# Evacuating transposed tiles on two engines, with one store of x per chunk, fewer halo copies and another load order

## The chip, the cores and the metric

One core of a Trainium2 chip runs the whole program. The metric is the device time of one execution in microseconds (us). The engines are named as in the profile: PE multiplies matrices and writes to PSUM, DVE (vector), ACT (scalar) and POOL (GpSimd) work element by element, and POOL and SP issue most DMAs. To evacuate a tile is to copy it out of PSUM. Most executions of a kernel lie within some 0.3% of each other, so every time below is set against runs of the kernel before on the same chip.

## The reference, cut to what matters

```python
x = causal_depthwise_conv(x_in, softmax(weight))   # 7 taps, 8 heads of 24 channels
theta = x @ w_theta                                # per token, 192 x 192
zr, zi = x * cos(theta), x * sin(theta)
y = w_tok_r @ zr + w_tok_i @ zi                    # over 4224 tokens: nearly all the work
u = x + y
out = u + relu(u @ w_ch)                           # per token, 192 x 192
```

Sizes: batch 8, 4224 tokens, 192 channels.

## The kernel before

The 4224 tokens are cut into 33 chunks of 128. A chunk is made ready as follows: load (`xw`), convolve on PE (tile `pc`), evacuate to `z`, transpose on PE (tile `tp`), evacuate to `uT`, multiply by `w_theta` (tile `v`), sines and cosines on ACT, products and sums on DVE. The token mixing (`y<-z,wt`) then runs over 11 chunks at a time. For the first 11 chunks, which I call the start, the chunks are made while PE already mixes those that are ready, so that each of PE, DVE and ACT can hold the others up. The parts that the change and the argument touch:

```python
    def evacuate(out, in_, by_dve=False):
        if by_dve:
            dve(nc.vector.tensor_copy(out=out, in_=in_))
        else:
            act(nc.scalar.activation(out=out, in_=in_, func=AT.Copy))

    def transposed(uT, u, gs, by_dve=False):
        tp = banks("tp", F16)                 # [128, 2, 1024] f16: one half of 2 KB for each g
        ...                                   # 6 transposes for each g of gs
        g = slice(gs[0], gs[-1] + 1)
        evacuate(uT[...][:, g, :], tp[:, g, 0 : 6 * P], by_dve)

    # Chunk.__init__: the 16 tokens of history of each of the four rows of a chunk
            for a in range(NQ):
                ...
                    nc.sync.dma_start(out=hist, in_=before.xw[lo + Q : lo + Q + HALO, h, :, :])
                ...
                nc.gpsimd.dma_start(out=self.xw[lo : lo + n, h, :, :], in_=x[...])
    # Chunk.conv, after the second half
                for a in range(NQ):
                    t0 = token(self.k, a)
                    nc.sync.dma_start(out=xs[t0 : t0 + Q, :], in_=self.x[a * Q : (a + 1) * Q, :])
    # Chunk.transpose
            transposed(self.xT, self.x, range(NG), self.k < 3)

    # the order of the first loads, all issued by POOL
    steps[0].load_rows()
    for m in (1, 2):
        steps[0].load_w(m)                    # token-mixing weights of the first step (tile st)
    load_chunk(2)
    for m in (1, 2):
        steps[1].load_w(m)
```

DVE transposes `st` into `wt` before PE can use it. `xs` is x in DRAM; `xr` is a row block of it that is read back and added to the partial sums `pv`, the first one at 591 us.

## Time and profile before

| What | Value | Where from |
|---|---|---|
| Time | 1449.16 us, 1445.77 to 1449.5, 3 runs | times |
| Span of the profile | 1446.4 us | page |
| Last PE wait of the start ends at | 104.61 us | timeline of PE |
| From there to the end of the span | 1341.8 us | difference |
| DVE waiting for an evacuation by ACT (`uT`), to 130 us | none | waits of DVE |

The prediction below shows the page and the waits.

### The profile page before, as it was taken

To read this page: it belongs to the slowest core of one execution; us is meant where nothing else is said; L and a number is where in the kernel's file an instruction comes from. 1 tells how busy PE (TensorE), PEld (TensorE's weight loads), DVE (VectorE), ACT (ScalarE), POOL (GpSimd) and SP (SyncE) were. 2 spreads that over 40 slices of the span, in tenths; PEclk is the share of its full clock that TensorE was granted. 3 is DMA by queue.
4 is the path that set the end of the run, shared out by engine and by line. 5 is a ranking of instruction groups with operands and counts; after the bars stand their busy time and mean duration, and the time that the engine had idled before them with its cause. 6 is when DMAs were issued, how large, how long until landed. Compare 5 with 4: busy or idle time off the path is not lost.

```text
span 1446.4 us, 23748 instructions
## 1 busy us (share of the span) xinstructions
PE 1416.3 (98%) x9809; PEld 887.9 (61%) x9809; DVE 979.2 (68%) x1051; ACT 315.5 (22%) x379; POOL 435.1 (30%) x655
## 2 busy tenths in 40 slices
PE   7899999999999999999999999999999999999997
PEld 5556666666666666666666666666666666666665
DVE  6893555545548777866666657877777667767686
ACT  5861101111134254000000004435210110010133
POOL 7431211111233232432433342233323123213120
PEclk9999999999999999999999999999999999999999
DMA  9986756465699998998899989999999999998893
GB/s 173 227 178 145 146 103 149 90 149 97 137 231 219 214 250 217 228 254 183 213 256 213 242 143 245 228 188 234 279 216 206 209 204 221 204 203 194 166 222 125
DMA packets 272029, 281.99 MB, mean 195 GB/s; under 512 B 106672, under 2 KB 240176, under 8 KB 271920
## 3 DMA queue, kind: packets, MB, share of 16 engines
q0 software_dynamic: 162464, 92.15, 48.4%
q1 hardware_dynamic: 71824, 178.88, 35.1%
q10 hardware_dynamic: 37632, 9.44, 4.1%
q8 instruction: 77, 1.26, 0.3%
q14 instruction: 32, 0.26, 0.1%
HBM read 245.49 MB, written 108.13 MB: 244 GB/s over the span
## 4 chain that ended last, share of the span: by engine, by line
PE 89%; DVE 4%; DMA 3%; POOL 2%; ACT 1%; issue 1%; SPq 0%; DVEq 0%; ACTq 0%; POOLq 0%
PE y L443 82%; PE v L141 5%; PE pc L210 1%; PE tp L165 1%; POOL st L323 1%; DMA xw<-in_x_dram 1%; DVE z L257 1%; DVE wt L336 1%; DVE pv L408 1%; ACT z L246 1%; DVE z L251 0%; DVE pv L476 0%; DVE wt L348 0%; POOL xw L197 0%; DMA xs<-z 0%
## 5 line engine op out<-in xcount | busy, mean ns | idle before, releaser
L443 PE MATMUL y<-z,wt 128*128 128x384 f16 x7656 | 1283.6, 326 | 10.6 <-DVE pv L408 7.5
L443 PEld LDWEIGHTS <-wt 128*128 128x128 f16 x7656 | 740.8, 98 | 488.6 <-issue 10.6
L408 DVE TENSOR_TENSOR pv<-y,pv 128x768 f32<-128x768 f32 x324 | 308.9, 954 | 323.6 <-PE y L443 282.8
L336 DVE STREAM_TRANSPOSE wt<-st 128x1408 f16<-128x1408 f16 (+7 forms) x224 | 327.8, 1465 | 48.5 <-PE y L443 39.0
L323 POOL DMA_DIRECT2D st<-in_moe_w_tok_r_dram x232 | 132.5, 578 | 466.1 <-DVE wt L336 461.0
L323 POOL DMA_DIRECT2D st<-in_moe_w_tok_i_dram x232 | 132.7, 578 | 404.4 <-DVE wt L336 388.9
L348 DVE TENSOR_TENSOR wt<-wt 128x1408 f16<-128x1408 f16 (+7 forms) x216 | 176.7, 818 | 40.8 <-PE y L443 38.4
L151 ACT ACTIVATE z<-pc 128x768 f16<-128x768 f32 x65 | 53.2, 819 | 387.2 <-PE pc L210 386.9
L151 ACT ACTIVATE ub<-pv 128x768 f16<-128x768 f32 x63 | 50.2, 835 | 333.0 <-DVE pv L408 310.4
L406 ACT ACTIVATE pv<-y 128x768 f32<-128x768 f32 x66 | 54.0, 819 | 282.0 <-PE y L443 282.0
L141 PEld LDWEIGHTS <-uT 128*128 128x128 f16 x1056 | 91.0, 98 | 25.8 <-issue 7.9
L386 POOL TENSOR_TENSOR pv<-pv,xr 128x1536 f32<-128x1536 f32 x24 | 74.5, 3105 | 68.6 <-DVE pv L476 22.1
L197 POOL DMA_DIRECT2D xw<-in_x_dram x132 | 76.4, 585 | 31.0 <-DMA xw<-xw 8.7
L476 DVE SCALAR_TENSOR_TENSOR pv<-v,pv 128x768 f32<-128x768 f32 x66 | 62.9, 954 | 27.5 <-PE v L141 27.1
L257 DVE TENSOR_TENSOR z<-z 128x768 f16<-128x768 f16 x132 | 73.4, 556 | 3.6
L151 ACT ACTIVATE uT<-tp 128x1536 f16<-128x1536 f16 (+1 forms) x48 | 58.2, 1215 | 74.4 <-PE tp L165 74.4
L246 ACT ACTIVATE z<-v,half_pi 128x768 f16<-128x768 f32 x66 | 59.8, 907 | 41.2 <-PE v L141 40.8
L251 DVE TENSOR_TENSOR z<-z 128x1536 f16<-128x1536 f16 x66 | 60.0, 947 | 7.5 <-ACT z L246 7.5
L141 PE MATMUL v<-wth,uT 128*128 128x192 f16 x528 | 55.0, 248 | 4.4 <-ACT z L246 3.0
L141 PE MATMUL v<-wch,uT 128*128 128x192 f16 x528 | 54.2, 246 | 2.1 <-DVE pv L476 1.2
L246 ACT ACTIVATE z<-v 128x768 f16<-128x768 f32 x66 | 53.4, 809 | 0.0
L210 PE MATMUL pc<-xw,bands 96*64 96x192 f16 x528 | 35.8, 258 | 2.6 <-ACT bands L625 1.1
(44 smaller groups left out, 142.4 us busy)
## 6 DMA issues: line engine op xcount, KB each, us to landing
part<-pv SPq DMA_DIRECT2D x79, 768.0 KB, 4.3
pv<-part SPq DMA_DIRECT2D x79, 768.0 KB, 6.1
out_dram<-pv SPq DMA_DIRECT2D x66, 384.0 KB, 4.3
st<-in_moe_w_tok_r_dram POOLq DMA_DIRECT2D x136, 176.0 KB, 5.5
st<-in_moe_w_tok_i_dram POOLq DMA_DIRECT2D x136, 176.0 KB, 5.1
xs<-z SPq DMA_DIRECT2D x132, 96.0 KB, 4.5
xw<-in_x_dram POOLq DMA_DIRECT2D x121, 96.0 KB, 6.1
xr<-xs SPq DMA_DIRECT2D x24, 384.0 KB, 3.7
```

Of the source, the lines that this page charges most:

```text
L141: pe(nc.tensor.matmul(v[:, k, b * D : (b + 1) * D], lhsT=tT[:, 3 * k + b + i, :], rhs=w[:, 2 * b + i, :], start=(i == 0), stop=(i == 1),))
L151: act(nc.scalar.activation(out=out, in_=in_, func=AT.Copy))
L197: nc.gpsimd.dma_start(out=self.xw[lo : lo + n, h, :, :], in_=x[:, t0 : t0 + n, :].rearrange("b s d -> s b d"),)
L246: act(nc.scalar.activation(**args))
L257: dve(nc.vector.tensor_tensor(out=z[:, o, :], in0=z[:, a, :], in1=z[:, b, :], op=ALU.subtract))
L323: pool(nc.gpsimd.dma_start(out=st[a * Q : (a + 1) * Q, 0:nb, :, 0:n] .rearrange("i r bt s -> i (r bt) s"), in_=w[self.tbs[0] * P : (self.t ...
L336: dve(nc.vector.transpose(self.w[name][:, 0 : self.n, :, :], self.st[int(name[1])][:, int(name[0]) - 1, :, 0 : self.n * Q] .rearrange("p b ...
L348: dve(nc.vector.tensor_tensor(out=self.w[name][:, 0 : self.n, :, :], in0=self.w[a][:, 0 : self.n, :, :], in1=self.w[b][:, 0 : self.n, :, : ...
L386: ins = pool(nc.gpsimd.tensor_tensor(out=self.pv[i], in0=self.pv[i], in1=self.xr[i], op=ALU.add))
L408: dve(nc.vector.tensor_tensor(out=o, in0=yv, in1=o, op=ALU.add))
L443: pe(nc.tensor.matmul(y[cn][:, q, 0:BH], lhsT=self.w[wn][:, c, :, :].rearrange("p bt i -> p (bt i)"), rhs=chunks[k].z[:, zn, q * BH : (q + ...
L476: dve(nc.vector.scalar_tensor_tensor(out=ub, in0=channel_mix(self.uT[i][:, 6 * g : 6 * g + 6, :], wch), scalar=0.0, in1=ub, op0=ALU.max, o ...
```

## The change

The intent: issue fewer DMAs (one 384 KB store of x instead of four of 96 KB, two halo copies per chunk instead of four), take the load of the channel weights out of the busy start, bring chunk 2 in earlier, and share the evacuation of each transposed x between ACT (first half) and DVE (second half) for chunks 0 to 10. Cut to its core:

```diff
-    xs = dram.tile([S, N], F16, name="xs")
+    xs = dram.tile([NK, P, N], F16, name="xs")
...
-    def transposed(uT, u, gs, by_dve=False):
+    def transposed(uT, u, gs, shared=False):
...
-        g = slice(gs[0], gs[-1] + 1)
-        evacuate(uT[...][:, g, :], tp[:, g, 0 : 6 * P], by_dve)
+        for g in [slice(g, g + 1) for g in gs] if shared else [slice(gs[0], gs[-1] + 1)]:
+            evacuate(uT[...][:, g, :], tp[:, g, 0 : 6 * P], shared and g.start == 1)
...
-            transposed(self.xT, self.x, range(NG), self.k < 3)
+            transposed(self.xT, self.x, range(NG), self.k < NW)
...
+            for lo in (0, WR) if before is not None else ():
+                nc.sync.dma_start(out=self.xw[lo : lo + HALO, :, :, :],
+                                  in_=before.xw[lo + Q : lo + Q + HALO, :, :, :])
...
-                for a in range(NQ):
-                    ...
-                    nc.sync.dma_start(out=xs[t0 : t0 + Q, :], in_=self.x[a * Q : (a + 1) * Q, :])
+                nc.sync.dma_start(out=xs[self.k, :, :], in_=self.x)
...
-            nc.sync.dma_start(out=self.xr[i], in_=xs[...])
+            for j in range(NQ):
+                a, k = divmod(NQ * self.tbs[i] + j, NK)
+                nc.sync.dma_start(out=self.xr[i][j * Q : (j + 1) * Q, :],
+                                  in_=xs[k, a * Q : (a + 1) * Q, :])
...
     steps[0].load_rows()
+    load_chunk(2)
     for m in (1, 2):
         steps[0].load_w(m)
-    load_chunk(2)
...                              # loads of wch moved into step NU - 2
```

## The prediction

> **What bounds the kernel now.** I read the page first, then the busy time by stretches, then the waits of PE up to 110 us, then the timelines of PE, ACT and DVE there.
>
> ```profile
> PE 1416.3 (98%) x9809; PEld 887.9 (61%) x9809; DVE 979.2 (68%) x1051; ACT 315.5 (22%) x379; POOL 435.1 (30%) x655
> PE 89%; DVE 4%; DMA 3%; POOL 2%; ACT 1%; issue 1%; SPq 0%; DVEq 0%; ACTq 0%; POOLq 0%
> ...
> 10.00:107.00 97.00, 83.83 (x748) 55.69 (x749) 82.19 (x123) 71.60 (x89) 46.65 (x83) 0.98 1.09 200
> 107.00:420.00 313.00, 313.00 (x1933) 188.37 (x1930) 157.52 (x138) 41.15 (x51) 65.44 (x115) 1.00 0.65 133
> ```
>
> The last two lines are stretches: length, then busy us of PE, weight loads, DVE, ACT and POOL, granted clock, DMA share. PE is the bound: from 107 to 420 us it never rests, and from 560 to 930 and 1030 to 1370 (same view) it does not either. The built programs have the same 19,620 PE instructions in the same order, so the change can only gain or lose PE idle time. There are four places of it: the start (13 us idle between 10 and 107), 0.7 us near 490, 2.1 us between 930 and 1030, 9 us after 1370. The last three are hardly touched: chunks from 11 on keep their one-piece ACT evacuation. So the case is decided in the start, where chunks 0 to 10 are made ready while DVE (82 of 97 us) and ACT (72 of 97) are nearly full too. What PE waits for before 110 us:
>
> ```profile
> PE y L443 <- DVE pv L408: 5.1, 5, 2.5
> PE y L443 <- ACT pv L406: 3.0, 3, 1.2
> PE v L141 <- ACT z L246: 2.5, 7, 0.6
> ...
> PE pc L210 <- DMA xw<-in_x_dram: 0.9, 1, 0.9
> PE v L141 <- ACT uT L151: 0.8, 1, 0.8
> ```
>
> Columns: us in total, times, longest. DVE costs 5.1 us, ACT 6.3, a DMA only 0.9. No wait names a store of x, a halo copy or the channel weights.
>
> **What the Trainium skill says.** "DMA: Bandwidth & Descriptors", Anatomy of one DMA, gives a fixed cost of about 2 us to a DMA, mostly completion: fewer, larger ones should save. The trace agrees that size hardly sets the time: a 96 KB store of x lands in 4.5 us, a 48 KB halo copy in 4.2, a 384 KB xr load in 3.7 (medians). The same page, Issuing engines are not separate DMA queues, says that issuing elsewhere saves only sequencer time; here SP is seldom what anyone waits for. "VectorE: DVE Perf Modes", The TRN2 errata, gives DVE 120 + elements/mode cycles at 0.96 GHz from PSUM: for 1536 at mode 2 that is 0.93 us, and the trace has 0.958. "Perfetto Trace Analysis", Tensor Engine Instruction, says ACT and DVE are strict FIFOs; the trace agrees where later DVE work stands behind a waiting product.
>
> **The change part by part.** The durations:
>
> ```profile
> L151 ACT ACTIVATE uT<-tp 128x1536 f16<-128x1536 f16 x30 | 43.7, 1458 | 51.8 <-PE tp L165 51.8
> ...
> L151 ACT ACTIVATE uT<-tp 128x768 f16<-128x768 f16 x18 | 14.5, 811 | 22.6 <-PE tp L165 22.6
> ...
> L149 DVE COPY uT<-tp 128x1536 f16<-128x1536 f16 x3 | 2.9, 958 | 3.5 <-PE tp L165 3.5
> ACT bands L625 <- DVE bands L622: 3.0, 1, 3.0
> ```
>
> *Store, halo, xr.* On SP 99 stores and 60 halo copies go, 72 xr loads come: 87 fewer. At 0.42, 0.53 and 0.32 us of issue that is 42 + 32 - 23 = 51 us less SP work. At most the 0.9 us DMA wait is on the path. Against it, the built order puts several early xr loads between stores and halo copies, where SP must wait for a store to land (4.5 us); halos have 2 us or more in hand. Value: 0 to -0.5 us.
>
> *Channel weights and chunk 2.* The weights leave POOL at 85 and 104 us, where POOL was waiting for DVE anyway; a 0.22 us memset leaves DVE's full stretch: -0.2. Chunk 2's load now stands before the first step's weights: those four i-weight DMAs are issued 2.3 us later, the DVE turns that need them come about 1.4 us later, and so does the second step's issue and the load of chunk 3, for which PE waits at 27.7 us. Against this, the halo of chunk 3 is earlier. Value: 0 to +1.
>
> *Two engines.* ACT saves 1.458 - 0.811 = 0.65 us for each of chunks 3 to 10. DVE gains a half: 0.958 less 384 cycles/0.96 GHz = 0.56 us (estimate from the page above), about 0.5 from start to start; eight of them are +4 us on DVE (chunks 0 to 2 had a whole one). If the halves ran side by side this would pay. But in the built program each of the 11 DVE halves waits for exactly the count that the ACT half of the same chunk raises. They write two parts of one tile, and are put in series, as the two writers of bands are in the last line above (ACT waited 3.0 us for DVE). And the DVE half stands ahead of the previous chunk's products. So DVE, a FIFO, now stops until ACT has come to its half:
>
> ```profile
> 32.85 0.96 DVE L251 TENSOR_TENSOR z<-z 128x1536 f16<-128x1536 f16 x1 [1.57 <-ACT z L246]
> 37.44 0.95 DVE L408 TENSOR_TENSOR pv<-y,pv 128x768 f32<-128x768 f32 x1
> 44.38 1.83 DVE L251 TENSOR_TENSOR z<-z 128x1536 f16<-128x1536 f16 x2 [1.52 <-ACT z L246]
> ...
> 33.37 0.85 ACT L406 ACTIVATE pv<-y 128x768 f32<-128x768 f32 x1
> 34.06 1.50 ACT L151 ACTIVATE uT<-tp 128x1536 f16<-128x1536 f16 x1
> 44.93 1.46 ACT L151 ACTIVATE uT<-tp 128x1536 f16<-128x1536 f16 x1
> ...
> 38.45 0.50 PE L443 MATMUL y<-z,wt 128*128 128x384 f16 x2 [0.78 <-DVE pv L408]
> ```
>
> Columns: start, length, what, and in brackets the idle time before it and who ended it. Walk it for chunk 3. The product starts at 32.85, when ACT's first sine is done. After the change it must follow ACT's second sine, the pv copy at 33.37, ACT's half (34.06 to 34.86) and DVE's half (to about 35.4): 2.5 us later. DVE is without a gap from the product to the eviction at 37.44, so that comes 2.5 us later, and PE, which waits for it at 38.45, resumes at 41.0. For chunk 4: product at 44.38; ACT's half 44.93 + 2.5 + 0.8 = 48.2, DVE's half to 48.8, product 4.4 us late, of which DVE's 1.8 us of idle before the next product take a part. Walking on this way to DVE's last catch-up, where PE waits till 104.61, I get DVE 5 to 6 us late: 65.5 us of its work remain from 32.85 (71.7 less 6.2 idle), plus 3.3 of new work, plus 2.5 of first delay, plus 4 to 6 of further waits for ACT, make 75 to 77 where there were 71.7: +3.6 to +5.6. The walk is pessimistic: where DVE is late anyway, ACT's half is done by then and costs no wait. With 2 us of waits in place of 4 to 6 it is +1.6.
>
> Sum: +1.6 to +5.6 for the halves, +0.3 for the DMAs and the order.
>
> **The rivals.** *A: it pays as intended.* ACT is 83 to 99% busy in each 10 us from 40 to 80 us and PE waited 6.3 us for it; 0.65 us less per chunk over seven chunks is up to 4.5 us, with DVE's 6.2 us of idle taking the new 4. It speaks for A that somebody kept this version, and that the three chunks done by DVE go well. Against: the serial wait, and DVE's backlog at the end of the start. Time: 1445 to 1447. *B: DVE becomes the bound of the start* (the walk above): 1451 to 1455. *C: nothing moves,* since what ACT gives DVE takes: 1448 to 1450. *D: a new wait later,* from four-part xr loads (1.3 us of SP issue instead of 0.3, one xr buffer): POOL's add has some 5 us in hand before the eviction that needs it, and PE has no idle there now; at worst +2.
>
> **Range and chances.** The three runs of before are 1445.8 to 1449.5, mean 1448.1. B alone with +4 gives 1452; A, which I hold for a third as likely as B with C between, pulls to 1451. I take 1451.0. The range reaches from A's middle, 1446.0, to B's far end, 1455.5. Two per cent is 29 us, more than the whole idle time of the start, so faster or slower by that is nearly excluded: 0.01 each.
>
> **What would show it.** Right: DVE uT halves with idle before them ended by ACT uT, 2 to 3 us in all for chunks 3 and 4; the first product after 35 us at 35 or later; the PE wait near 38 grown to about 3 us; PE busy from 10 to 107 below 83.8 and the last PE wait of the start later than 104.6; nothing new between 107 and 1370. Wrong: halves that start together, ACT waits of PE shrunk with no growth of DVE's, the unbroken stretch beginning before 104; or a change of more than 2 us after 420, which would make a DMA or the xr loads the cause.

## More of the kernel before

The build may hoist an instruction that has nothing to wait for.

## The result, and the profile after

The changed kernel took 1459.9 us in the median (1459.7 to 1460.36, 4 runs); before took 1448.92 (1445.77 to 1449.5, 4 runs). The ratio is 1.0081, 95% interval 1.0063 to 1.0098: slower by 0.8%, which is within 2%. A ratio here is not quite the ratio of the medians that I quote. The predicted direction was right, but the 11 us lie outside the range. All outputs are right.

The page of the changed kernel, its engine line and its chain of work by engine:

```profile
PE 1419.8 (97%) x9809; PEld 888.7 (61%) x9809; DVE 980.5 (67%) x1059; ACT 312.9 (21%) x382; POOL 437.6 (30%) x657
PE 89%; DVE 6%; DMA 2%; POOL 1%; issue 1%; ACT 1%; DVEq 0%; POOLq 0%; ACTq 0%
```

The same PE instructions; DVE has a larger part of the chain (6% against 4%). The busy time by stretches, with the columns that the prediction explains:

```profile
10.00:107.00 97.00, 78.51 (x713) 52.15 (x714) 76.03 (x119) 68.99 (x92) 42.95 (x76) 0.96 1.02 192
107.00:420.00 313.00, 309.76 (x1890) 185.53 (x1888) 160.62 (x144) 40.55 (x50) 66.14 (x117) 0.99 0.63 129
110.00:120.00 10.00, 6.76 (x24) 3.12 (x23) 7.82 (x9) 0.00 (x0) 2.29 (x4) 0.66 0.52 70
```

PE has lost 5.3 us of busy time in the start, and so has DVE its 6.2: an engine that was given more work became less busy, so it must wait more. The last line also shows a granted clock of 0.66 around the end of the start. The waits of PE up to 130 us, then of DVE:

```profile
PE y L459 <- DVE pv L424: 11.0, 6, 4.4
PE pc L226 <- ACT z L258: 2.9, 2, 1.5
...
PE y L459 <- ACT pv L422: 1.7, 2, 1.1
```

```profile
DVE uT L163 <- ACT uT L165: 15.1, 8, 3.3
```

The wait for DVE's evictions of y has doubled from 5.1 to 11.0 us, and the new wait that leads to it is named: DVE's half of `uT` waits for ACT's half, 15.1 us in all. The groups of instructions by form show that the halves themselves are as short as planned, 0.547 and 0.816 us:

```profile
L165 ACT ACTIVATE uT<-tp 128x768 f16<-128x768 f16 x29 | 23.6, 816 | 24.9 <-PE tp L179 24.9
L163 DVE COPY uT<-tp 128x768 f16<-128x768 f16 x11 | 6.0, 547 | 15.1 <-ACT uT L165 15.1
```

The timelines around chunk 3, and the end of the start, answer to those shown of before (ACT, then DVE, then PE):

```profile
35.41 0.85 ACT L422 ACTIVATE pv<-y 128x768 f32<-128x768 f32 x1
36.10 0.86 ACT L165 ACTIVATE uT<-tp 128x768 f16<-128x768 f16 x1
...
37.00 0.56 DVE L163 COPY uT<-tp 128x768 f16<-128x768 f16 x1 [2.44 <-ACT uT L165]
37.47 0.95 DVE L263 TENSOR_TENSOR z<-z 128x1536 f16<-128x1536 f16 x1
...
42.47 0.95 DVE L424 TENSOR_TENSOR pv<-y,pv 128x768 f32<-128x768 f32 x1
...
43.48 0.82 PE L459 MATMUL y<-z,wt 128*128 128x384 f16 x2 [4.40 <-DVE pv L424]
...
113.70 12.49 PE L459 MATMUL y<-z,wt 128*128 128x384 f16 x58 [3.24 <-DVE pv L424]
```

Read them as one chain. ACT's half stands behind ACT's sines and a copy of pv; DVE's half stands behind ACT's half; DVE's product stands behind its half; the eviction at 42.47, which was at 37.44, stands behind the product; PE, which resumed at 38.45, resumes at 43.48. Two of these 5 us were there already: the transposes of chunk 3 begin at 33.70 on PE rather than 31.65. The start's last PE wait ends at 113.70, 9.1 us later than before. From there to the end of the span it is 1344.9 us, 3.1 more than before; 420 to 1370 us is practically unchanged. So the whole loss is made before 120 us. The 3.1 us are the clock's. With narrower stretches it is seen to step: it is 0.50 for 6.83 us from 112.79 us on, and PE is busy for 5.92 us of these, at half speed, which loses 3.0 us. The first two lines are of the changed kernel, the last two of e8, an experiment below with the same wait of 3.24 us:

```profile
109.38:112.79 3.41, 1.08 (x7) 0.43 (x5) 3.20 (x5) 0.00 (x0) 0.00 (x0) 1.00 0.61 89
112.79:119.62 6.83, 5.92 (x19) 2.85 (x20) 4.86 (x6) 0.00 (x0) 2.29 (x4) 0.50 0.52 67
...
108.73:112.14 3.41, 2.15 (x14) 1.07 (x11) 3.27 (x5) 0.00 (x0) 0.00 (x0) 1.00 1.05 143
112.14:115.55 3.41, 1.44 (x9) 0.90 (x10) 3.31 (x5) 0.00 (x0) 0.00 (x0) 1.00 0.01 2
```

The part on why the prediction was right or wrong comes back to these lines.

### The profile page after: what moved, and what is told of

It reads as the page before. It is cut to its first block, busy times and chain, and to the rows that moved or that the text cites. A ratio compares the mean times of both kernels' runs of the same rounds, so it can differ in the third digit from the quotient of the medians.

```text
span 1458.6 us, 23574 instructions
## 1 busy us (share of the span) xinstructions
PE 1419.8 (97%) x9809; PEld 888.7 (61%) x9809; DVE 980.5 (67%) x1059; ACT 312.9 (21%) x382; POOL 437.6 (30%) x657
## 3 DMA queue, kind: packets, MB, share of 16 engines
q8 instruction: 77, 1.26, 0.3%
## 4 chain that ended last, share of the span: by engine, by line
PE 89%; DVE 6%; DMA 2%; POOL 1%; issue 1%; ACT 1%; DVEq 0%; POOLq 0%; ACTq 0%
PE y L459 82%; PE v L155 5%; DVE z L269 1%; PE pc L226 1%; PE tp L179 1%; DMA xw<-in_x_dram 1%; DVE z L263 1%; DVE pv L424 1%; DVE wt L348 1%; DVE wt L360 1%; POOL xw L213 1%; DVE pv L492 0%; POOL st L335 0%; ACT z L258 0%; DMA xw<-xw 0%
## 5 line engine op out<-in xcount | busy, mean ns | idle before, releaser
L165 ACT ACTIVATE uT<-tp 128x768 f16<-128x768 f16 (+1 forms) x51 | 55.5, 1090 | 76.6 <-PE tp L179 76.6
```

## The experiments

Fifteen kernels ran. "End of the start" is the moment at which PE's last wait there ends, in the one profiled run; the times are medians. Both are needed: the first has no noise from the rest of the program but is a single run, the second is what counts.

| Run | What is in it | Time, us | Ratio to before (95%) | End of the start, us |
|---|---|---|---|---|
| before | | 1448.92 | 1 | 104.61 |
| changed | all | 1459.90 | 1.0081 (1.0063 to 1.0098) | 113.70 |
| e1 | split alone | 1456.35 | 1.0050 (1.0035 to 1.0066) | 111.08 |
| e2 | all but the split | 1452.95 | 1.0025 (1.0010 to 1.0040) | 109.11 |
| e3 | all, two PSUM tiles | 1463.30 | 1.0093 (1.0076 to 1.0110) | 120.42 |
| e4 | all, DVE's half first | 1452.16 | 1.0023 (1.0008 to 1.0038) | 107.96 |
| e5 | e2, old load order | 1450.63 | 1.0007 (0.9991 to 1.0024) | 106.28 |
| e6 | load order alone | 1450.09 | 1.0002 (0.9987 to 1.0017) | 106.62 |
| e7 | all, chunks 1 and 8 whole | 1459.62 | 1.0067 (1.0050 to 1.0084) | 114.74 |
| e8 | all, two SBUF tiles | 1460.41 | 1.0077 (1.0056 to 1.0099) | 114.11 |
| e9 | e2, xr with its step | 1456.93 | 1.0048 (1.0033 to 1.0063) | 108.50 |
| e10 | e5, xr with its step | 1450.98 | 1.0007 (0.9992 to 1.0022) | 103.48 |
| e11 | all, DVE first, as e10 | 1453.02 | 1.0018 (0.9998 to 1.0039) | 104.54 |
| e12 | e10, whole tiles shared | 1453.65 | 1.0027 (1.0012 to 1.0042) | 107.37 |
| e13 | e2, xr after the start | 1452.99 | 1.0020 (1.0005 to 1.0035) | 110.17 |
| e14 | e5, xr after the start | 1448.53 | 1.0001 (0.9985 to 1.0018) | 104.19 |
| e15 | e14 with the split, DVE first | 1448.66 | 0.9996 (0.9981 to 1.0012) | 105.81 |

A caution on single profiles: the 32 small matmuls that make the convolution bands took 2.6 us in most profiles and 1.6 us in those of e5, e6, e11 and e15, so these began about 1.1 us ahead of the others. Their starts may look up to that much better than they are.

### e1 and e2: the split alone, and everything else alone

e1 is the kernel before with only this:

```diff
-        g = slice(gs[0], gs[-1] + 1)
-        evacuate(uT[...][:, g, :], tp[:, g, 0 : 6 * P], by_dve)
+        for g in [slice(g, g + 1) for g in gs] if shared else [slice(gs[0], gs[-1] + 1)]:
+            evacuate(uT[...][:, g, :], tp[:, g, 0 : 6 * P], shared and g.start == 1)
...
-            transposed(self.xT, self.x, range(NG), self.k < 3)
+            transposed(self.xT, self.x, range(NG), self.k < NW)
```

> The kernel before with nothing but the two-engine evacuation of chunks 0 to 10; stores, halo copies, xr loads, order of loads and channel weights as before. Serial theory (each DVE half waits for the ACT half of its chunk, and DVE's queue stands meanwhile): this alone is the loss, 1458 to 1461 us against 1449, DVE waits for ACT's uT of 13 to 17 us before 115 us. Rival 1 (the loss is from the DMA parts, such as early xr loads in SP's queue and the four i-weight loads behind chunk 2): 1448 to 1452. Mixed: between.

e2 is the changed kernel with the evacuation of before (the same lines the other way round).

> The changed kernel with the evacuation of before (chunks 0 to 2 whole on DVE, later ones whole on ACT); all its other parts stay. Serial theory: 1447.5 to 1450, within 1 us of before. Rival 1 (DMA parts): 1455 to 1460. If the parts help by a shorter SP queue: 1444 to 1447.

Against 1449.15 us of before in that call, e1 is 7.2 us slower and e2 3.8: both causes are real, as neither interval reaches 1. That their sum, 11.0, is just the whole change is in part chance: in the profiles the starts end 6.5 and 4.5 us later, which makes 11.0, where the changed kernel's ends 9.1 us later and loses 3.1 us to the clock. Of the expectations, e1 came out as the mixed case, and e2 fell between its theory and its rival. The waits of e1 up to 130 us, and PE's line that answers to 38.45 of before:

```profile
PE y L443 <- DVE pv L408: 11.1, 7, 4.0
...
DVE uT L149 <- ACT uT L151: 15.2, 8, 3.1
...
41.26 0.82 PE L443 MATMUL y<-z,wt 128*128 128x384 f16 x2 [3.98 <-DVE pv L408]
```

The serial wait belongs to the split and not to the DMA parts. Of its 15.2 us, 6.5 fall on chunks 0 to 2, where they cost the path next to nothing (ACT's half of chunk 3 starts at 34.29 against 34.06), and 8.7 on chunks 3 to 10.

### e3, e4 and e8: what puts the halves in series, and what it costs which way round

e3 gives each half its own PSUM tile; e8 gives each half its own SBUF tile and leaves the PSUM tile whole; e4 evacuates DVE's half first:

```diff
# e3
-        tp = banks("tp", F16)
+        if shared:
+            tps = [banks("tp", F16), banks("tp", F16)]
+        else:
+            tps = [banks("tp", F16)] * 2
...
# e8
-            self.xT = turned()
+            self.xT = [turned(), turned()] if self.k < NW else [turned()] * 2
# e4
-        for g in [slice(g, g + 1) for g in gs] if shared else ...:
+        for g in [slice(g, g + 1) for g in reversed(gs)] if shared else ...:
```

> The changed kernel with the transposes of a shared chunk in two PSUM tiles instead of one; same PE and DVE order, same halves; in the build each DVE half now waits for PE alone. Serial theory: the 15.1 us of DVE waits for ACT's uT are gone and the time falls to 1445 to 1451 (the small cost: both PSUM buffers of the pool are taken by one chunk). Rival 2 (it is the 4 us of new DVE work, whoever it waits for): no less than 1455. If ACT's relief pays as it was meant: below 1447.

> The changed kernel with the two halves written to two separate SBUF tiles; the PSUM tile that both read is still one. In the build each DVE half still waits for the ACT half. Theory (the common PSUM tile is what puts the halves in series): 1458.5 to 1461 us, DVE waiting about 15 us for ACT's halves, as in the changed kernel. Rival (the prediction's reason, two writers of one tile): the waits are gone and the time falls to 1453 us. It is also a second look at the drop of PE's granted clock to 0.66 between 110 and 120 us: if long idle of PE brings it on, it is there again.

> The changed kernel with the two halves in the other order: DVE's half first, ACT's half waits for DVE's. Same work on each engine. Serial theory: DVE's 15 us of waits go, and ACT waits instead where DVE is late (after some 60 us), so better than the change but not as good as the kernel before: 1450 to 1456. Rival 2 (new DVE work is the cost): 1458 to 1461 as the change.

With two SBUF tiles nothing changes (1460.41 us), and the waits of DVE still have this line:

```profile
DVE uT L163 <- ACT uT L165: 15.7, 8, 3.2
```

With two PSUM tiles the wait of DVE for ACT is gone, but the pool of these PSUM tiles has two places: the second `tp` takes the place that theta's `v` still holds, so PE now waits for ACT's sines before it can transpose at all. The waits of PE in e3:

```profile
PE tp L182 <- ACT z L261: 11.3, 10, 1.4
```

So e3 exchanged one wait for another: its start ended 6.7 us later than the changed kernel's, and its ratio is 1.0093 against 1.0081, which the intervals do not tell apart. The pair e3 and e8 shows which tile the series comes from: two readers of one PSUM tile are ordered by the build, two writers of one SBUF tile were not the reason. It does not show what truly concurrent halves would be worth, as e3's expected gain never came. That stays open.

e4 turns the series round. Now ACT waits for DVE, and this is the waits of ACT:

```profile
ACT uT L165 <- DVE uT L163: 9.3, 6, 3.0
```

9.3 us of waiting remain, yet the time falls to 1452.16 us, that of e2, where there is no split. The wait itself is not the price; the price is that it fell on DVE, whose evictions PE waits for.

### e7: do the exchanged PSUM places matter?

In the changed build DVE's half stands later in the order at chunks 1 and 8, and there theta's tile takes the PSUM place of the convolution's tile, not of the transposed one. PE's new waits of 1.5 and 1.4 us at 24.66 and 85.63 us follow from it. e7 leaves these two chunks unsplit:

```diff
...                     # transposed() takes by_dve again, for a whole tile on DVE
-            transposed(self.xT, self.x, range(NG), self.k < NW)
+            transposed(self.xT, self.x, range(NG), self.k < NW and self.k not in (1, 8), self.k == 1)
```

> The changed kernel with chunk 1 evacuated whole by DVE and chunk 8 whole by ACT, the two chunks at which the build gave theta's tile the banks of the convolution instead of those of the transposition; nine chunks stay split. Theory: the swaps cost about 2 us each on PE (waits of 0.5 and 1.5 us near 22 and 25 us, 0.35 and 1.4 near 83 and 86), so this run is 1454.5 to 1457 us and those waits are gone. Rival: the time is set by DVE's serial waits, and the swaps only shift where PE waits. Then it is 1458 to 1460 us, as two of eleven serial waits are small.

The theory fell: the two waits are gone, PE's wait for the evictions grew from 11.0 to 12.4 us, and the time is 1459.62. PE's wait had only moved from one place to another while DVE set the pace.

### e5 and e6: the load order, first attempt

```diff
# e5 against e2                          # e6 against before: the reverse
-    load_chunk(2)
     for m in (1, 2):
         steps[0].load_w(m)
+    load_chunk(2)
```

> The changed kernel with the whole-tile evacuation of before, as in e2, and also with chunk 2's load back behind the first step's weight loads. Theory: the 3.8 us that e2 lost come from that order alone, because the weights of the first step land late and DVE's turns of them (7.1 us of waiting in e2, none before) hold DVE. Then this run is 1448 to 1450 us, and DVE waits for no weights in the start. Rival: the 3.8 us come from the single store, the halo copies or the four-part xr loads. Then it stays at 1452 to 1454 us.

> The kernel before with nothing changed but chunk 2's load moved ahead of the first step's weight loads. Theory (the order costs): 1451.5 to 1454 us, with DVE waiting 6 to 9 us for the weights in the start. Rival (stores, halos, xr cost): 1448 to 1450 us.

Each of the two lies within the noise of before, so neither expectation was met as a whole: without the changed order the DMA parts cost little, but the changed order alone with before's stores costs little too. Against the expectation DVE still waited 2.1 us for i-weights (the tile `moe_w_tok_i`) in the start of e5, at 17.15 us. (The 7.1 us that the expectation names for e2 are 2.8 us in its start and 4.3 us at 122 us, after it; before has such a late wait too, 3.1 us at 116 us.) In e6 DVE waited 3.2 us for them, and its profile shows the order at work as the pair e13 and e14 will below: DVE turns them at 19.42 us instead of 16.36, and the start ends 2.0 us later than before's, with bands that came 1.1 us sooner. So e6 does not clear the order; its four times, at -0.13% to +0.17%, cannot show a cost of that size. e5 has a wait that none of the theories had. The queue of SP, then PE:

```profile
17.70 4.19 SPq L393 DMA_DIRECT2D xr<-xs  x2
21.99 1.14 SPq L198 DMA_DIRECT2D xw<-xw  x2
...
27.52 0.24 PE L226 MATMUL pc<-xw,bands 96*64 96x192 f16 x1 [2.64 <-DMA xw<-xw]
```

The first xr load, needed only near 590 us, now consists of four parts, each of which needs one chunk's store only. The build hoists three of them to 17.70 and 28.80 us (before's one load, which needs the stores of four chunks, came at 82.6 us), SP waits for the store to land before it can issue the part (4.19 us for two), and the halo copy of chunk 3 stands behind it.

### e9 to e12: holding the xr load back, first attempt

```diff
# e9 (on e2), e10 (on e5); e11 is e10 with the split, DVE first
-                nc.sync.dma_start(out=self.xr[i][...], in_=xs[...])
+                ins = nc.sync.dma_start(out=self.xr[i][...], in_=xs[...])
+                if self.t == first_add:
+                    tc.add_manual_dep(ins.ins, last["dve"].ins.name, SYNC, reason="pace")
# e12: e10, and
-            transposed(self.xT, self.x, range(NG), self.k < 3)
+            transposed(self.xT, self.x, range(NG), self.k < 3 or self.k in (4, 6, 8, 10))
```

> The changed kernel with the whole-tile evacuation of before, as in e2, in the changed load order, but the four parts of the first xr load, which the build had put among the halo copies and stores of the start (SP waited 8.4 us there in e5 for stores to land), are tied to the step that needs them, some 590 us in. Theory (the early xr loads are a part of what the DMA changes cost): 1449.5 to 1451.5 us, half or more of e2's 3.8 us gone. Rival (the order alone makes the weights late, with or without xr): 1452 to 1454 us. The DVE wait for the weights of 6 to 8 us should stay in either case.

> As e9, with chunk 2's load behind the first step's weight loads again, as before: the single store, the halo copies of a chunk in two and the channel weights in a quiet step are then all that is changed. Theory: nothing of cost is left, PE's wait of 2.6 us for a halo copy (e5) is gone: 1447.5 to 1450 us, no different from the kernel before by more than 0.1%. Rival: the halo copies, which wait for the whole of the chunk ahead, or the larger stores cost: 1450.5 to 1453 us.

> All of the change, with three repairs: DVE's half goes first and ACT's half waits for it (e4), chunk 2's load is behind the weights again, the early xr loads are tied to their step. Theory (in series, the split costs when DVE waits and saves when ACT waits, as DVE is the fuller engine): 1446 to 1449 us, PE's waits for ACT smaller than before's 6.3 us, a ratio of 0.998 to 1.000. Rival (DVE's 4 us of new work set the end of the start whichever goes first): 1450 to 1453 us.

> The same intent without any split: the tile of chunks 0 to 2, 4, 6, 8 and 10 is evacuated whole by DVE, the others whole by ACT; store, halo copies and weights as in e10. About as much new DVE work (4 times 0.96 us) as eight halves, but no half that waits for another. Theory (the serial wait is the loss, not the amount of DVE work): 1446 to 1450 us. Rival (DVE's work is the loss): 1451 to 1454 us.

The times missed what the theories expected (those of e10 and e12 lie where their rivals had them, e11's at the edge), but they can't decide, and the fault was in my repair: tied to its step, the xr load stood ahead of a load of partial sums on SP, and PE was busy for 944.2 to 944.9 us between 420 and 1370 us where before has 947.1. All four carry these 2 to 3 us, and the profiles of e9, e10 and e11 some 1.7 us more, since the clock fell to 0.50 for 3.41 us in that wait of PE, near 610 us. What they show of the start holds: with the old order and no early xr load it ends at 103.48 us, with the changed order at 108.50. e12 adds four whole evacuations to DVE, 4 x 0.96 = 3.8 us of work and no half that waits for another, and the start ends 3.9 us later than in e10. That suggests that DVE's time is the start's time, but it is not clean: DVE also waited longer for transposes (5.9 us up to 130 us, against 2.8 in e10), and e4 and e15, which put about as much new work on DVE in halves, end their starts 1.2 us before e2's and 1.6 us after e14's.

### e13 to e15: holding it back until the end of the start

```diff
-                    tc.add_manual_dep(ins.ins, last["dve"].ins.name, SYNC, reason="pace")
+                    tc.add_manual_dep(ins.ins, mark[0].ins.name, SYNC, reason="pace")
...
     ready[0] = NK
+    mark.append(last["dve"])
```

> e2 (DMA parts alone, changed order), with the first xr load held back until the end of the start. Theory (the order is most of the DMA cost, the early xr load little of it while the order is changed): 1451.5 to 1454.5 us, the last wait of the start ending near 108.5 us as in e9, PE busy from 420 to 1370 us at 947 as before. Rival (the xr load is most of it): 1448.5 to 1450.5 us.

> The same in the load order of before. Theory: nothing of cost remains, 1447 to 1449.5 us, the last wait of the start ending at 103 to 105 us as in e10. Rival (halo copies or stores cost): over 1450.5 us.

> All of the change with DVE's half first, the old load order, and the first xr load held back until the end of the start. Theory (with these repairs the split is worth nothing, since DVE's new work takes what ACT's shorter half gives): 1448 to 1451 us, within 0.15% of the kernel before. Rival (it pays): 1444 to 1447 us. Rival (it costs): 1451.5 to 1455 us.

All three times came as the theory had it (e13's start ended at 110.17 us, not near 108.5), and PE is back at 947.1 us between 420 and 1370. e13 and e14 differ in the load order alone: 1452.99 against 1448.53 us, 4.5 us by the medians and 3.3 us by the means of six runs each. The timelines show how an order of DMA issues becomes 4 us on PE. First e14 (old order): POOL's issue of the i-weights, DVE's turn of them, PE's convolution of chunk 3.

```profile
10.07 1.14 POOL L335 DMA_DIRECT2D st<-in_moe_w_tok_i_dram  x2
...
16.37 0.44 DVE L348 STREAM_TRANSPOSE wt<-st 128x256 f16<-128x256 f16 x1
...
27.02 0.52 PE L226 MATMUL pc<-xw,bands 96*64 96x192 f16 x7 [0.43 <-DMA xw<-in_x_dram]
```

The same three in e13 (changed order):

```profile
13.08 2.28 POOL L335 DMA_DIRECT2D st<-in_moe_w_tok_i_dram  x4 [0.38 <-DMA xw<-in_x_dram]
...
20.37 0.45 DVE L348 STREAM_TRANSPOSE wt<-st 128x256 f16<-128x256 f16 x1 [3.52 <-DMA st<-in_moe_w_tok_i_dram]
...
31.45 0.85 PE L226 MATMUL pc<-xw,bands 96*64 96x192 f16 x7 [3.10 <-DMA xw<-in_x_dram]
```

The i-weights are issued 3.0 us later, DVE's turn comes 4.0 us later, and DVE, being a FIFO, holds everything behind it. Part of this is taken up: e14's DVE waits 1.58 us for the next tile at 19.72 us, so in e13 that tile comes 2.35 us later. The second step's weights need the buffers that this turn frees, so POOL issues the last of those at 22.12 instead of 19.18, and chunk 3's load follows them. PE meets both delays at 31.45 us, 4.4 us later than in e14. e14 also answers for the rest: one store, two halo copies and the quiet load of the channel weights are worth nothing measurable (ratio 1.0001). e5 against e14 puts the early xr load at 2.1 us of the start in the old order (one profile of each); of the time it is not clear of noise (1.0007 against 1.0001). In the changed order e2 and e13 have the same 1453 us, since chunk 3's halo copies are then issued at 13.36 us, ahead of it.

e15 is the whole change with its three faults mended, and is no faster than before or than e14; in the profiles its start ends 1.6 us later than e14's. No version that I tried beats the kernel before.

## Why the prediction was right or wrong

**Where the case is decided: right.** From the end of the start on, before takes 1341.8 us, e1 1341.8 and e2 1342.3. Nothing slowed down after 420 us.

**Rival B, DVE as the bound of the start: right, and larger than its own range.** DVE's half took 0.547 us on average against the 0.56 estimated, PE's wait near 38 us appeared, and the walk for chunk 3 can be checked in e1, where nothing else is changed: PE was to resume at 41.0 and resumed at 41.26. The first delay and the further waits were put at 6.5 to 8.5 us in all, and the waits measured 8.7 for chunks 3 to 10. The end of the start was to be 3.6 to 5.6 us late and was 6.5 late; the time rose by 7.2 us.

**The step that failed first** is the discount after that walk: "The walk is pessimistic: where DVE is late anyway, ACT's half is done by then and costs no wait." This let the sum sink to +1.6, and then, mixed with rival A, to +2. In e1 it held for only three of the eight chunks: those at 63.52, 80.46 and 88.15 us had no wait. The other five did: after chunk 3's wait of 2.11 us came 2.88, 1.28, 2.09 and 0.37 us, 6.6 us where the walk had 4 to 6 and the discount 2. The walk should have been believed at its upper end.

**The step that failed second** is the term of the DMA parts, "+0.3 for the DMAs and the order". It measured +3.8 us (e2). The chain was the right one: weights issued later, DVE's turns later, the next weights and chunk 3 later. But the first turn of the i-weights came 2.5 us later in the changed kernel itself (18.90 us against 16.36), 4.2 us in e2 and 4.0 in e13 against e14, where the prediction had 1.4. I valued the delay as if DVE's slack took it up: there was 1.58 us of it, and the rest reached PE, above all through the load of chunk 3 (2.1 us later on PE in the changed kernel, 3.7 in e2, 4.4 in e13). It is the term that was mis-sized most: by 3.5 us, against 1.6 for the halves if the walk is taken at its upper end (+5.6, measured +7.2).

**The clock, not predicted at all.** In the profiled runs 3.1 us of the 12.2 between the spans came after the start's last wait, and the lines in the part on the result show them: a granted clock of 0.50 for 6.83 us. The traces show when it falls. In each of them the clock changes at whole multiples of 3.41 us from its other changes. In the 3.41 us before the fall PE had been idle for 2.33 us (3.41 less 1.08 busy, the first line) in the changed kernel, and for 2.76, 2.46 and 2.31 us in e7, e6 and e11, which fell too at the end of the start (the last two in waits of only 2.46 and 2.77 us). In the other thirteen profiles no such stretch there has more than 1.97 us of idle, and none fell: in e8 the wait of 3.24 us is split into 1.26 and 1.97 us, in e1 that of 3.39 us into 1.83 and 1.56. From the wait to the end e8 has 1342.0 us. So in these traces what counts is how a wait falls on these stretches, and not its length alone. No experiment set out to test this, and I claim no sharp bound: before 50 us, falls came after as little as 1.63 us of idle. The medians contain the clock in part: e1's two runs at a mean clock of 0.998 took 1454.65 and 1454.96 us, its two at 0.994 took 1457.74 and 1458.71, and the four of the changed kernel stood at 0.993 to 0.995.

**The reason given for the series was wrong.** "They write two parts of one tile" is refuted by e8; e3 points to the one PSUM tile that both read. The consequence drawn from it was right.

**Store, halo copies and channel weights: right** in that they are worth nothing (e14, +0.01%). The early xr loads were seen, but "halos have 2 us or more in hand" was true only in the changed order; in the old order PE waited 2.6 us for one (e5), and the profiled start ended 2.1 us later than e14's. The 2 us of fixed cost that the prediction quotes are fitted, in the section named, to DMAs that GpSimd issues; these are issued by SP, and no run here measures such a cost for them.

**Rival A, that it pays,** fails even when mended: e15 equals e14. That DVE's new work takes what ACT's shorter half gives is the likely reason, but no run separates the two. Nothing is seen of rival C or D: the loss is clear of noise, and none of it comes after 420 us.

## What to carry to other kernels

Before an evacuation is split between two engines, look in the build for a semaphore that orders the halves: in series the split gained nothing here (whether it pays side by side is not shown). If they must be in series, let the fuller engine go first, so that the wait falls on the other. The busy share of an engine does not tell what a wait on it costs: ask which later instruction in its queue somebody else waits for. And when loads are reordered or cut into parts, follow the one that comes later through its consumer's queue, and look for loads that the build can now hoist.

## What the Trainium skill lacked or had wrong

- "PSUM — Partial Sum Buffer", section "PSUM bank collisions raise a hardware error", wants two engines kept apart per bank and quadrant of 32 partitions. The two halves lie in two different banks of 2 KB and would need nothing of it, but the build orders the two readers of the tile: 8 waits, 15.1 us. The page does not warn of a wait that is coarser than its rule. Separate tiles removed it and brought another for PSUM places (e3: 11.3 us).
- "TensorE: Matmul & The Clock Gate", section "What's actually happening", gives an idle window of about 3.4 us, free-running, before the clock falls to half. The clock steps at multiples of 3.41 us and falls to 0.50. The window need not be idle throughout. At the end of the start it fell after windows with 2.31 to 2.76 us of idle, and stayed after all with at most 1.97. So a wait of 2.46 us (e6) cost 1.7 us of clock, and one of 3.39 us (e1), split between two windows, cost none.
- No page has what a DMA's place in the issue order can cost: 3.0 us later on POOL became 4.4 us on PE at chunk 3 and 4.5 us of the median time, 3.3 of the mean (e13 against e14).
